# Two linear-attention blocks behind one gate: how B's reciprocals reach the partitions that scale with them

## The chip, the cores and the metric

The kernel runs on one core of one Trainium2 chip. The metric is the device time of one execution in microseconds; the times shown are medians of several runs. A core has a matrix engine (TensorE; PE in the profile, its weight loads PEld), a vector engine (VectorE, DVE), a scalar engine (ScalarE, ACT), GpSimd (POOL) and SyncE (SP), which here only issues DMA transfers. All five run their own instruction streams in order and wait for each other by semaphores.

## The reference

Two blocks A and B of linear attention work on the same x (2048 rows of 640), each with 32 heads of 20 columns, and a gate mixes them row by row:

```python
x = A_x
g = _sigmoid((x * gate_w).sum(-1, keepdims=True))
a = _A_ref(x, A_wqkv, A_wo)
b = _B_ref(x, B_wqkv, B_wo)
return g * a + (1 - g) * b

# each block, for every head:
pq, pk = phi(q), phi(k)      # phi(t) = where(t > 0, t + 1, exp(t)) + 1e-6
kv  = einsum("bhsd,bhse->bhde", pk, v)
z   = einsum("bhsd->bhd", pk)
num = einsum("bhqd,bhde->bhqe", pq, kv)
den = einsum("bhqd,bhd->bhq", pq, z)[..., None] + 1e-6
o   = num / den              # then all heads side by side, @ wo
```

Inputs and output are bf16.

## The kernel before, in words

The rows are cut in 16 tiles of 128. The kernel never forms v or the attention output: it computes G = x^T phi(k), from it kv = wv^T G for each head, and M = kv wo (640 by 640, one for each block, called M_A and M_B), so that the output is the sum over both blocks of (phi(q) / den, weighted by the gate) times M. phi(q) lies transposed in `pqT[0]` (A) and `pqT[1]` (B): five chunks of 128 columns by 2048 rows. Its columns are dealt out in a mixed order, so that partition p of every chunk belongs to head p // 4. One row of reciprocals per head therefore serves four neighbouring partitions.

**The reciprocals.** `Den.mm` multiplies phi(q) by the heads' sums of phi(k). The result has one partition for each of four groups of 512 rows and each of 32 heads. `ln`, `rec` and `ex` make `rT` of it, 128 partitions by 512, the gate divided by the denominator. `R` holds the same numbers spread out: partition p has the 2048 values of head p // 4, in four parts j of 512 rows. `scale(b, m, part)` multiplies chunk m of `pqT[b]` by R on VectorE, over all rows or over `part`. There is one R: A's values are in it first, and B's overwrite them after A's last scaling, `scale(0, 4)`.

- For A, `norm_load` (L976) stores rT four times over to DRAM (`r_rows`, 512 KB) and loads it back into R. It follows `ex2` in a list of steps called PLAN, at about 65 us.
- For B, `norm_spread` (L983) does it on the chip: four matmuls with a 0/1 matrix `spread` as weights (L988), and two ScalarE copies from PSUM into R (L992).

**Around it.** `g_strassen(1, ...)` (L736) computes G of block B by the Strassen-Winograd scheme from seven products `g_prod`, each with 16 matmuls. Instructions of VectorE, ScalarE and SyncE are written between the products by hand, in the order in which these engines execute them. `m_a(g, slot)` and `m_b(g, banks)` make six row blocks of M_A and M_B; each is copied from PSUM and stored to DRAM (`m_rows`, L878). M_A is then loaded back in the layout that the last product wants (L764), M_B in two loads (`m_load`, L899). M_A's tile `M[0]` is also the place where its blocks stand before they are stored. `load_wo(1, ...)` loads B's output weights in three transfers (L1121 twice, L1124).

**The last product** is again a Strassen-Winograd scheme, over rows 0 to 1023 (`SH` = 1024) and the rest, A and B, and the column halves of M. `p_diff(rows)` makes D3, the difference of A's two row halves; `p_sums(rows, ks)` makes sums of A's and B's scaled halves (k = 1: lower halves A + B, in place in `pqT[0]`; 2 and 4: into xT). `tm_first` makes TM[0] = M_A's right half minus its left, `m_sum(k)` TM[1] to TM[3], which need M_B. `part[0..3]` are row quarters of 256 rows within each half. Eight `Pair`s of row tiles run products `p1` to `p7`: p1 needs A's upper rows and M_A; p5 needs sum 1 and TM[0]; p2 needs B's scaled upper rows and M_B; p7 needs D3 and TM[2]; p6 needs sum 2 and TM[1]; p4 needs B's scaled lower rows and TM[3]; p3 needs sum 4 and M_B.

SyncE's queue before, from 116 us on: stores of M_A's blocks 0 to 5, the load of M_A (it waits for those stores to land), three loads of wo, stores of M_B's blocks 0 to 5, two loads of M_B, and the stores of the output.

Of the kernel before, what the change touches and what calls it, by code (L numbers as in the profile page):

```python
# [9 lines left out]
P = 128  # L10
FP32 = mybir.dt.float32
BF16 = mybir.dt.bfloat16
# [3 lines left out]
S, D, H = 2048, 640, 32  # L16
# [39 lines left out]
def kernel(  # L56
# [52 lines left out]
    def ps(name, slot=None):  # L109

        return banks(ps_raw(name, slot))
# [11 lines left out]
    zE = persist.tile([P, 2 * D], BF16, name="zE")  # L123
    E4 = zE[:, D:2 * D]
    maskE = persist.tile([P, HF], BF16, name="maskE")
    spread = persist.tile([P, P], BF16, name="spread")
    R = persist.tile([P, 4, HB], BF16, name="R")
    kv6 = [persist.tile([P, D], BF16, name="kvA6")[:], zE[:]]
    lift = persist.tile([P, 1], FP32, name="lift")
# [27 lines left out]
    scratch = ctx.enter_context(tc.tile_pool(name="scratch", bufs=1, space=bass.MemoryType.DRAM))  # L157
    m_rows = scratch.tile([D, D], BF16, name="m_rows")
    g_rows = scratch.tile([2 * ST, P], FP32, name="g_rows")
    r_rows = scratch.tile([4, P, HB], BF16, name="r_rows")  # L160

    wq_dram = [A_wqkv.rearrange("(c p) f -> p c f", p=P), B_wqkv.rearrange("(c p) f -> p c f", p=P)]
    wo_dram = [A_wo, B_wo]
# [37 lines left out]
    for r in range(4):  # L201
        rows = slice(32 * r, 32 * r + 32)
        nc.gpsimd.tensor_copy(out=I4[rows], in_=ident[rows, rows])
    nc.gpsimd.tensor_copy(
        out=spread[:].rearrange("p (h t) -> p h t", t=TW), in_=I4[:, :, None].to_broadcast([P, H, TW])
    )
    nc.gpsimd.memset(maskE[:], 1.0)
    for lo in range(0, HF, K6):
        part = maskE[:, lo:min(lo + K6, HF)]
# [526 lines left out]
    def g_strassen(b, main, second, spare, rest=None):  # L736

        x11, x12 = [xn[:, k:k + hc, 0:ic] for k in (0, hc)]
        x22 = xn[:, hc:ST, ic:2 * ic]
        b11 = pk[:, 0:hc, 0:HF]  # L740
        b21, b22 = [pk[:, hc:ST, n * HF:(n + 1) * HF] for n in range(2)]
        lo, hi = GT

        def temp(name):
            return work.tile([P, 2, HF], FP32, tag="osb", name=name, bufs=3)

        def add(dst, pt, sb):
            nc.vector.tensor_tensor(out=dst, in0=pt[:, :, 0:HF], in1=sb[:], op=ALU.add)

        even, odd = ps("gs0", main), ps("gs1", second)  # L750
        sel = []
        g_prod(even, x11, b11, True)
        nc.scalar.copy(out=odd[:, :, 0:HF], in_=even[:, :, 0:HF])
        if b == 0:
            rest()
            zr = z_rows(0, spare)
            sq_sum(1, 0)
            g_prod(even, x12, b21, False)
            nc.scalar.copy(out=lo[:, 0:2, :], in_=even[:, :, 0:HF])
            sq_sum(2, 0)  # L760
            x_sum(3)
        else:
            m_a(5, 2)
            nc.sync.dma_start(out=M[0][:], in_=m_rows[:].rearrange("(p m) d -> p m d", m=DT))  # L764
            load_wo(1, nc.sync)
            scale(0, 3)
            zr = z_rows(1, spare)
        g_prod(odd, SX[2], TK[b][2], False, lambda: sel.append(z_pass(b, zr)))
        u2 = temp("u2")
        nc.scalar.copy(out=u2[:], in_=odd[:, :, 0:HF])  # L770
        if b == 1:
            scale(0, 4)
            p_diff(part[0])
            rts = rec_pass(b, sel[0], 2)
            k_sum(1, 1)
            for rows in part[1:3]:
                p_diff(rows)
            g_prod(even, x12, b21, False)
            nc.scalar.copy(out=lo[:, 0:2, :], in_=even[:, :, 0:HF])
            norm_spread(b, rts, (2, spare))  # L780
        else:
            k_sum(0, 1)
            norm_load(rec_pass(b, sel[0], 2))
            x_sum(4)
            for k in (3, 4):
                sq_sum(k, 0)
            tq_sums(1, (0, 1))
        g_prod(odd, SX[3], TK[b][3], False)
        u3 = temp("u3")
        nc.scalar.copy(out=u3[:], in_=odd[:, :, 0:HF])  # L790
        if b == 1:
            for rows, ms in ((slice(0, SH), (0, 1)), (slice(SH, S), (0, 1))):
                for m in ms:
                    scale(b, m, rows)
        even = ps("gs0", main)
        g_prod(even, SX[1], TK[b][1], True)
        add(hi[:, 2:4, :], even, u3)
        if b == 0:
            tq_sums(1, (2, 3))
        else:  # L800
            scale(b, 2)
            scale(b, 3)
        g_prod(odd, x22, TK[b][4], False)
        nc.scalar.copy(out=lo[:, 2:4, :], in_=odd[:, :, 0:HF])
        for ns in ((0, 1),) if b == 0 else ((0,), (1,)):
            g_prod(even, SX[4], b22, False, None, ns)
            for n in ns:
                nc.vector.tensor_tensor(out=hi[:, n, :], in0=even[:, n, 0:HF], in1=u2[:, n], op=ALU.add)
            if b == 1 and ns == (0,):
                rest()  # L810

    def z_rows(b, slot=None):

# [66 lines left out]
    def m_a(g, slot):  # L880

        pt = ps("mA", slot)
        to = m_block(0, g, cells(pt), M[0][:, g, :] if g < DT else None)
        n = to.shape[0]
        nc.scalar.copy(out=to.rearrange("p (b n) -> p b n", b=2), in_=pt[:n, :, 0:HF])
        m_store(g, to)
# [43 lines left out]
    def rec_pass(b, zsel, slot):  # L930

        d = Den(b, lambda: ps(f"den{'AB'[b]}", slot)[:, 0, :])
        d.mm(zsel)
        for go in (d.ln, d.rec, d.ex) if b == 0 else (d.ln,):
            for n in range(2):
                go(n)
        if b == 1:
            for n in range(2):
                d.rec(n)
                d.ex(n)  # L940
        return d.rT
# [4 lines left out]
    def p_diff(rows):  # L946

        up = slice(SH + rows.start, SH + rows.stop)
        add_rows(D3[:, :, rows], pqT[0][:, :, rows], pqT[0][:, :, up], ALU.subtract)
# [12 lines left out]
    def tm_first(cs):  # L962
        add_rows(TM[0][:, cs], M[0][:, cs, HF:D], M[0][:, cs, 0:HF], ALU.subtract)
# [9 lines left out]
        else:  # L973
            add_rows(TM[3][:], b[:, :, lo], TM[1][:], ALU.subtract)

    def norm_load(rT):  # L976

        nc.sync.dma_start(
            out=r_rows[:].rearrange("j (h t) n -> (j h) t n", t=TW), in_=rT[:, None, :].to_broadcast([P, TW, HB])
        )  # L980
        nc.sync.dma_start(out=R[:], in_=r_rows[:].rearrange("j p n -> p j n"))

    def norm_spread(b, rT, slots):  # L983

        pts = [ps(f"ex{'AB'[b]}", s) for s in slots]
        for j in range(4):
            rows = slice(32 * j, 32 * j + 32)
            nc.tensor.matmul(  # L988
                pts[j // 2][:, j % 2, :], lhsT=spread[rows, :], rhs=rT[rows, :], start=True, stop=True,
            )  # L990
        for jj in range(2):
            nc.scalar.copy(out=R[:, 2 * jj:2 * jj + 2, :], in_=pts[jj][:])  # L992

    def scale(b, m, part=slice(0, S)):

        rec = R[:].rearrange("p j n -> p (j n)")
        nc.vector.tensor_tensor(out=pqT[b][:, m, part], in0=pqT[b][:, m, part], in1=rec[:, part], op=ALU.mult)
# [119 lines left out]
    def load_wo(b, eng):  # L1117
        wo_sb[b] = wpool.tile([P, 2, 3, D], BF16, tag="wo", name=f"wo{'AB'[b]}")
        halves = wo_dram[b].rearrange("(h r) f -> h r f", h=2)
        for h in range(2):  # L1120
            eng.dma_start(  # L1121
                out=wo_sb[b][:K6, h, 0:2], in_=halves[h, 0:2 * K6].rearrange("(j p) f -> p j f", p=K6)
            )
        eng.dma_start(out=wo_sb[b][:HF - 2 * K6, :, 2], in_=halves[:, 2 * K6:HF].rearrange("h p f -> p h f"))  # L1124
# [68 lines left out]
    with tc.manual_schedule():  # L1193
# [166 lines left out]
        for name in PLAN.split():  # L1360
            steps[name]()
            if name == "ex2":
                norm_load(den.rT)
        t1 = wpool.tile([P, hc, HF], BF16, tag="wk", name="T1")
        TK[1][1] = t1[:]
        for k in (3, 2, 4):
# [12 lines left out]
        def kv_low():  # L1379
            kv = cells(ps("kvB", 2))  # L1380
            kv_mm(1, kv, range(3))
            kv_mask(1, kv, 0, 2)
            kv_mask(1, kv, 2, 3)
            tm_first(slice(0, 3))

        g_strassen(1, 1, 0, 3, kv_low)
        new_stage(None)
# [11 lines left out]
            kv_mm(1, [None, acc["x"][g > 3]], [g], (2, 3, 4, 0, 1))  # L1399
        for g in range(3, 6):  # L1400
            kv_mask(1, [None, acc["x"][g > 3]], g, g + 1)
        pairs[4].p1(acc["w"][0], (0, 1))
        m_b(3, [acc["w"][1], acc["x"][0]])
        pairs[4].p1(acc["w"][0], (2,))
# [2 lines left out]
        pairs[4].p1(acc["w"][0], (3, 4))  # L1407
        pairs[4].p1_out()
        m_load(0, 3, nc.sync)
        m_load(3, 6, nc.sync)  # L1410
        tm_first(slice(3, DT))
        scale(1, 4)
        for rows, ks in ((0, (1,)), (1, (1,)), (2, (1,)), (0, (2, 4))):
            p_sums(part[rows], ks)
        for k, to in ((5, None), (6, acc["x"][0]), (7, acc["w"][1]), (2, acc["z"][0]), (3, acc["z"][1])):
            pairs[k].p1(to)
        held["p5"] = wpool.tile([P, 4, HF], FP32, tag="wv", name="p5s")
        pairs[0].p1()
        pairs[2].p5(spare[0])
        pairs[3].p5(acc["w"][1])  # L1420
        pairs[1].p1()
        pairs[4].p5(spare[0])
        pairs[5].p5(acc["z"][1])
        for p in pairs[0:2]:
# [2 lines left out]
        inner = ctx.enter_context(late_pool("inner"))  # L1427
        acc["y"] = [bank(inner, f"oy{n}") for n in range(2)]
        TM[3] = wpool.tile([P, DT, HF], BF16, tag="wk", name="TM3")
        p_sums(part[1], (2, 4))  # L1430
        p_diff(part[3])
        for k in (2, 1, 3):
            m_sum(k)
        for p in pairs[0:2]:
            p.p2()
            p.c11()
        for p in pairs[0:2]:
            p.p7()
            p.p6()
            p.c22()  # L1440
        pairs[0].p4()
        pairs[0].p3()
        later = {1: (2, (2,)), 2: (2, (4,)), 4: (3, (2,)), 5: (3, (4,))}
# [51 lines left out]
```

## Time and profile before

| | us |
|---|---|
| runs | 182.61, 183.02, 183.47 |
| median | 183.02 |
| the profiled execution | 182.66 |
| its span on the core | 180.9 |
| TensorE busy | 176.9 |
| TensorE weight loads (beside the matmuls) | 117.6 |
| VectorE busy | 150.6 |
| ScalarE busy | 104.8 |
| GpSimd busy | 5.0 |

The profile is of one execution. A line of its timeline has the start in us from the beginning of the span, the duration in us, the engine, the line of the kernel, the operation, out<-in by the program's names, shapes and the count of instructions merged, and in brackets the idle time before it with what ended it. A line of waits has the total, the count and the longest. A line of DMA issues has the KB of each and the median time from issue to landing. SPq stands for an issue by SyncE; its duration is that of the issue, not of the transfer. In a line of windows the columns are the stretch, its length, busy us of PE, PEld, DVE, ACT and POOL with counts, TensorE's granted clock, the DMA engines' share and GB/s. A tile's name may be that of its storage: `zE` holds B's kv blocks, `SQ` holds D3, `xT` some of the sums.

### The profile page before, as it was taken

The numbers are of one execution on the slowest core, as the hardware profiler recorded it, in microseconds if no ns is written. First come the engines' busy times: TensorE is split into PE (matmuls) and PEld (weight loads), VectorE is DVE, ScalarE is ACT, GpSimd is POOL, SyncE is SP. The second block draws the span as 40 slices with busy tenths as digits, with TensorE's granted clock in tenths as the row PEclk, the third lists the DMA queues.
The fourth block names the chain that finished last, engine by engine and source line by source line (L and its number), as shares of the span: only waits on it lengthen the run. The fifth ranks groups of instructions, "written<-read, shape, count | busy, mean of one in ns | idle before, by whom it ended". The sixth has DMA issues, their size and how long they took to land.

```text
span 180.9 us, 3378 instructions
## 1 busy us (share of the span) xinstructions
PE 176.9 (98%) x1282; PEld 117.6 (65%) x1282; DVE 150.6 (83%) x275; ACT 104.8 (58%) x212; POOL 5.0 (3%) x21
## 2 busy tenths in 40 slices
PE   7999999999999999999999999999999999999993
PEld 2666656655666677676666566766678777777772
DVE  0478988999899999998888889987988988687764
ACT  2066579975884434547777695863814755466210
POOL 8300000000000000000000000000000000000000
PEclk9999999999999999999999999999999999999999
DMA  5995448985002634032000000043901560222132
GB/s 176 286 184 92 93 111 264 366 178 150 31 0 85 209 111 135 0 82 99 5 0 0 0 0 5 23 135 101 277 10 42 163 163 0 100 105 90 72 132 89
DMA packets 21602, 18.85 MB, mean 104 GB/s; under 512 B 9298, under 2 KB 21074, under 8 KB 21586
## 3 DMA queue, kind: packets, MB, share of 16 engines
q1 hardware_dynamic: 20722, 17.82, 35.5%
q10 hardware_dynamic: 864, 0.82, 1.5%
q8 instruction: 10, 0.16, 0.4%
q14 instruction: 6, 0.05, 0.1%
HBM read 11.86 MB, written 4.80 MB: 92 GB/s over the span
## 4 chain that ended last, share of the span: by engine, by line
PE 96%; DMA 2%; DVE 1%; issue 0%
PE kA L313 12%; PE kB L313 11%; PE gs L731 9%; PE q L500 9%; PE gs L1251 9%; PE qA L366 7%; PE oy L1008 6%; PE oz L1008 5%; PE ox L1008 5%; PE ow L1008 4%; PE q L431 4%; PE gB L701 2%; PE gA L701 2%; DMA xn<-in_A_x_dram 2%; PE q L366 2%; PE kB L500 1%
## 5 line engine op out<-in xcount | busy, mean ns | idle before, releaser
L313 PEld LDWEIGHTS <-xT 128*128 128x128 bf16 x300 | 28.9, 97 | 14.1 <-DVE xT L271 0.3
L313 PE MATMUL kA<-wkA,xT 128*128 128x320 bf16 (+1 forms) x160 | 23.4, 299 | 0.0
L313 PE MATMUL kB<-wkB,xT 128*128 128x320 bf16 x140 | 20.8, 299 | 0.0
L524 ACT ACTIVATE e<-kB 128x640 bf16<-128x640 f32 (+1 forms) x17 | 11.4, 676 | 9.5 <-PE kB L313 5.7
L282 ACT ACTIVATE e<-kA 128x640 bf16<-128x640 f32 x16 | 11.3, 715 | 7.8 <-PE kA L313 7.8
L524 ACT ACTIVATE e<-q 128x512 bf16<-128x512 f32 x18 | 10.3, 596 | 6.7 <-PE q L500 3.8
L537 DVE SCALAR_TENSOR_TENSOR pk<-kB,e 128x640 bf16<-128x640 f32 (+1 forms) x17 | 13.2, 782 | 0.9
L366 PE MATMUL qA<-xT,wqA 128*128 128x512 bf16 x60 | 13.4, 379 | 0.0
L290 DVE TENSOR_SCALAR e<-e 128x640 bf16<-128x640 bf16 (+2 forms) x28 | 9.6, 346 | 4.0 <-ACT e L282 3.8
L530 DVE TENSOR_SCALAR e<-e 128x640 bf16<-128x640 bf16 (+2 forms) x30 | 9.9, 332 | 2.3 <-ACT e L524 2.3
L366 PEld LDWEIGHTS <-wqA 128*128 128x128 bf16 x64 | 7.5, 117 | 5.9
L1071 ACT COPY u<-ox 128x320 f32<-128x320 f32 x8 | 3.4, 425 | 11.4 <-PE ox L1008 11.4
L1008 PEld LDWEIGHTS <-xT 128*128 128x128 bf16 x85 | 8.1, 98 | 2.9
L1008 PEld LDWEIGHTS <-pqTA 128*128 128x128 bf16 x85 | 8.0, 98 | 2.8
L1013 DVE TENSOR_TENSOR osb<-oz,u 128x320 bf16<-128x320 f32 (+2 forms) x18 | 8.0, 453 | 2.2 <-PE oz L1008 1.8
L1008 PEld LDWEIGHTS <-pqTB 128*128 128x128 bf16 x80 | 7.7, 98 | 3.1 <-DMA MB<-m_rows 0.2
L500 PE MATMUL q<-xT,wqB 128*128 128x512 bf16 x32 | 9.0, 379 | 0.0
L301 DVE SCALAR_TENSOR_TENSOR pk<-kA,e 128x640 bf16<-128x640 f32 x10 | 8.2, 822 | 0.9
L282 ACT ACTIVATE e<-qA 128x1024 bf16<-128x1024 f32 x6 | 6.2, 1027 | 4.4 <-PE qA L366 4.4
L701 PEld LDWEIGHTS <-xn 128*128 128x128 bf16 x64 | 6.2, 98 | 3.0
L1251 PEld LDWEIGHTS <-xn 128*128 128x128 bf16 x64 | 6.1, 98 | 3.1 <-DVE xn L944 0.4
L731 PEld LDWEIGHTS <-xn 128*128 128x128 bf16 x64 | 6.1, 98 | 2.9 <-issue 0.7
(212 smaller groups left out, 368.5 us busy)
## 6 DMA issues: line engine op xcount, KB each, us to landing
out_dram<-osb SPq DMA_DIRECT2D x14, 160.0 KB, 1.8
xn<-in_A_x_dram SPq DMA_DIRECT2D x3, 640.0 KB, 6.2
wvA<-in_A_wqkv_dram SPq DMA_DIRECT2D x1, 800.0 KB, 10.3
wkB<-in_B_wqkv_dram SPq DMA_DIRECT2D x1, 800.0 KB, 4.6
wqB<-in_B_wqkv_dram SPq DMA_DIRECT2D x1, 800.0 KB, 6.6
wvB<-in_B_wqkv_dram SPq DMA_DIRECT2D x1, 800.0 KB
MA<-m_rows SPq DMA_DIRECT2D x1, 800.0 KB, 6.4
MB<-m_rows SPq DMA_DIRECT2D x2, 400.0 KB, 4.1
```

Source lines behind the costliest of these rows:

```text
L282: nc.scalar.activation(out=to, in_=part, func=ACT.Exp)
L290: nc.vector.tensor_scalar(self.e, self.e, 1.0, EPS, op0=ALU.min, op1=ALU.add)
L313: nc.tensor.matmul(pt[:, hf, 0:n], lhsT=xT[:, c, i * P:(i + 1) * P], rhs=wk[b][:, c, hf * HF:hf * HF + n], start=(c == 0), stop=(c == DT - 1),
L366: nc.tensor.matmul(dst, lhsT=mixed(wq[b][:, c, :], m), rhs=xT[:, c, n * HB:(n + 1) * HB], start=first, stop=last,)
L500: nc.tensor.matmul(dst, lhsT=left(c), rhs=right(c), start=first and k == 0, stop=last and k == len(cs) - 1, skip_group_check=not first,)
L524: nc.scalar.activation(out=self.part(self.e, k), in_=self.srcs[k](), func=ACT.Exp)
L530: nc.vector.tensor_scalar(self.e, self.e, 1.0, EPS, op0=ALU.min, op1=ALU.add)
L537: nc.vector.scalar_tensor_tensor(out=self.part(self.dst, k), in0=src(), scalar=1.0 + EPS, in1=self.part(self.e, k), op0=ALU.add, op1=ALU.max,)
L701: nc.tensor.matmul(pt[:, hf, 0:HF], lhsT=xn[:, i, c * P:(c + 1) * P], rhs=pk[:, i, hf * HF:(hf + 1) * HF], start=(i == 0), stop=(i == ST - 1),
L731: nc.tensor.matmul(pt[:, n, 0:HF], lhsT=left[:, i, n * P:(n + 1) * P], rhs=right[:, i, :], start=(first and i == 0), stop=(i == hc - 1), s ...
L1008: nc.tensor.matmul(dst, lhsT=left[:, c, r0:r0 + P], rhs=right[:, c, :], start=(first and c == 0), stop=(c == DT - 1), skip_group_check=not ...
L1251: nc.tensor.matmul(dst[n], lhsT=left[:, i, n * P:(n + 1) * P], rhs=right[:, i, :], start=(first and i == 0), stop=(i == hc - 1), skip_grou ...
```

## The change

- `norm_store` stores rT once (128 KB) and `norm_load` reads it back in four loads, one for each group of 512 rows; each row of DRAM is read by four partitions. A and B have their own DRAM scratch. Both blocks use this; the spread matrix, its matmuls and copies are gone.
- In `g_strassen(1, ...)`, B's wo is loaded ahead of M_A, and the store and loads of the reciprocals follow M_A's load on SyncE's queue.
- `scale` for B is by row halves: the upper halves of chunks 0 to 2 follow the fourth G product, chunk 3 the kv masks, chunk 4 the masks of the second half; the lower halves of all five stand after the loads of M_B.
- `p_diff(part[3])` and the whole of `tm_first` move into `g_strassen(1, ...)`, ahead of the fourth G product.
- M_B is read back in three loads: blocks 0 to 2, blocks 3 and 4, block 5.
- The order of the sums changes (quarters 1, 2, 0 for k = 1), `p_sums(part[1], ...)` moves behind `m_sum`, and the P1 products of pairs 0 and 1 now both stand ahead of the P5 products. Pair 3's P5 uses another bank.

```diff
@@ -157,7 +156,7 @@
-    r_rows = scratch.tile([4, P, HB], BF16, name="r_rows")
+    r_rows = [scratch.tile([4, H, HB], BF16, name=f"r_rows{b}") for b in "AB"]
@@ -761,8 +757,8 @@
             m_a(5, 2)
+            load_wo(1, nc.sync)
             nc.sync.dma_start(out=M[0][:], in_=m_rows[:].rearrange("(p m) d -> p m d", m=DT))
-            load_wo(1, nc.sync)
             scale(0, 3)
@@ -771,16 +767,17 @@
             p_diff(part[0])
-            rts = rec_pass(b, sel[0], 2)
+            norm_store(1, rec_pass(b, sel[0], 2))
+            norm_load(1, range(4))
             k_sum(1, 1)
...
-            norm_spread(b, rts, (2, spare))
...
@@ -789,17 +786,16 @@
         if b == 1:
-            for rows, ms in ((slice(0, SH), (0, 1)), (slice(SH, S), (0, 1))):
-                for m in ms:
-                    scale(b, m, rows)
+            p_diff(part[3])
+            tm_first(slice(0, DT))
         even = ps("gs0", main)
         g_prod(even, SX[1], TK[b][1], True)
         add(hi[:, 2:4, :], even, u3)
...
-            scale(b, 2)
-            scale(b, 3)
+            for m in (0, 1, 2):
+                scale(b, m, slice(0, SH))
         g_prod(odd, x22, TK[b][4], False)
...
                 rest()
+                scale(b, 3, slice(0, SH))
@@ -973,23 +970,16 @@
+    def norm_store(b, rT):
+
+        nc.sync.dma_start(out=r_rows[b][:].rearrange("j h n -> (j h) n"), in_=rT[:])
+
+    def norm_load(b, js):
+
+        for j in js:
+            nc.sync.dma_start(
+                out=R[:, j, :], in_=r_rows[b][j][:, None, :].to_broadcast([H, TW, HB])
+            )
...
@@ -1381,7 +1372,6 @@
             kv_mask(1, kv, 2, 3)
-            tm_first(slice(0, 3))
@@ -1399,6 +1389,7 @@
             kv_mask(1, [None, acc["x"][g > 3]], g, g + 1)
+        scale(1, 4, slice(0, SH))
         pairs[4].p1(acc["w"][0], (0, 1))
@@ -1407,18 +1398,19 @@
         m_load(0, 3, nc.sync)
-        m_load(3, 6, nc.sync)
-        tm_first(slice(3, DT))
-        scale(1, 4)
-        for rows, ks in ((0, (1,)), (1, (1,)), (2, (1,)), (0, (2, 4))):
+        m_load(3, 5, nc.sync)
+        m_load(5, 6, nc.sync)
+        for m in range(DT):
+            scale(1, m, slice(SH, S))
+        for rows, ks in ((1, (1,)), (2, (1,)), (0, (1,)), (0, (2, 4))):
             p_sums(part[rows], ks)
...
-        pairs[0].p1()
+        for p in pairs[0:2]:
+            p.p1()
         pairs[2].p5(spare[0])
-        pairs[3].p5(acc["w"][1])
-        pairs[1].p1()
+        pairs[3].p5(acc["z"][0])
...
-        p_sums(part[1], (2, 4))
-        p_diff(part[3])
         for k in (2, 1, 3):
             m_sum(k)
+        p_sums(part[1], (2,))
...
             p.c22()
+            if p.i == 0:
+                p_sums(part[1], (4,))
```

More of the change, by code (lines that the diff above doesn't have):

```diff
@@ L125 @@
     maskE = persist.tile([P, HF], BF16, name="maskE")
-    spread = persist.tile([P, P], BF16, name="spread")
     R = persist.tile([P, 4, HB], BF16, name="R")
@@ L203 @@
         nc.gpsimd.tensor_copy(out=I4[rows], in_=ident[rows, rows])
-    nc.gpsimd.tensor_copy(
-        out=spread[:].rearrange("p (h t) -> p h t", t=TW), in_=I4[:, :, None].to_broadcast([P, H, TW])
-    )
     nc.gpsimd.memset(maskE[:], 1.0)
@@ L779, in g_strassen @@
             nc.scalar.copy(out=lo[:, 0:2, :], in_=even[:, :, 0:HF])
-            norm_spread(b, rts, (2, spare))
         else:
             k_sum(0, 1)
-            norm_load(rec_pass(b, sel[0], 2))
+            norm_store(0, rec_pass(b, sel[0], 2))
+            norm_load(0, range(4))
             x_sum(4)
@@ L974, in m_sum @@
             add_rows(TM[3][:], b[:, :, lo], TM[1][:], ALU.subtract)
[L976 to L989, printed above, removed]
-            )
-        for jj in range(2):
-            nc.scalar.copy(out=R[:, 2 * jj:2 * jj + 2, :], in_=pts[jj][:])
+    def norm_store(b, rT):
[4 more added lines that the diff above has]
+                out=R[:, j, :], in_=r_rows[b][j][:, None, :].to_broadcast([H, TW, HB])
+            )
     def scale(b, m, part=slice(0, S)):
@@ L1362 @@
             if name == "ex2":
-                norm_load(den.rT)
+                norm_store(0, den.rT)
+                norm_load(0, range(4))
         t1 = wpool.tile([P, hc, HF], BF16, tag="wk", name="T1")
```

## The prediction

> **What bounds the kernel now.** I read the page first: busy times, then the chain of work that ended last.
>
> ```profile
> span 180.9 us, 3378 instructions
> PE 176.9 (98%) x1282; PEld 117.6 (65%) x1282; DVE 150.6 (83%) x275; ACT 104.8 (58%) x212; POOL 5.0 (3%) x21
> ...
> PE 96%; DMA 2%; DVE 1%; issue 0%
> ```
>
> TensorE makes up 96% of the chain, and "issue", the time in which it waits for nothing visible, is 0%. The kernel is bound by TensorE from end to end. An edit can gain only by taking TensorE work away, and it loses when it makes TensorE wait. So I then read the timeline around the edited lines (105 to 154 us), to see which work of VectorE and of the DMA queues ends just before TensorE needs it.
>
> ```profile
> 122.35 0.31 SPq L878 DMA_DIRECT2D m_rows<-m  x1
> ...
> 124.08 0.35 SPq L764 DMA_DIRECT2D MA<-m_rows  x1
> ...
> 124.52 0.88 SPq L1121 DMA_DIRECT2D woB<-in_B_wo_dram  x2
> ...
> 125.45 1.27 SPq L1124 DMA_DIRECT2D woB<-in_B_wo_dram  x1
> ...
> 125.48 2.35 PE L731 MATMUL gs<-pk,xn 128*128 128x320 bf16 x16
> ...
> 126.56 0.78 ACT L928 ACTIVATE rT<-d 128x256 bf16<-128x256 f32 x2
> ...
> 127.76 0.39 PE L988 MATMUL exB<-rT,spread 32*128 32x512 bf16 x4
> ...
> 128.09 2.35 PE L731 MATMUL gs<-xT,xn 128*128 128x320 bf16 x16
> 128.22 1.55 DVE L944 TENSOR_TENSOR SQ<-pqTA 128x1280 bf16<-128x1280 bf16 x2
> ...
> 129.69 2.49 DVE L997 TENSOR_TENSOR pqTB<-pqTB,R 128x1024 bf16<-128x1024 bf16 x4
> ...
> 130.27 2.34 PE L731 MATMUL gs<-T,S 128*128 128x320 bf16 x16
> ```
>
> **What is removed.** The four matmuls of L988 and two ScalarE copies. Sixteen G matmuls without them start 2.18 us before the next sixteen (128.09 to 130.27); with them it is 2.61 us (125.48 to 128.09). So they cost TensorE **0.43 us**, and that is all the change can gain: everything else on TensorE is only reordered. The two copies and GpSimd's copy for the spread matrix lie beside TensorE and count nothing.
>
> **A's spread.** One store of 128 KB and four loads take the place of a 512 KB store and one 512 KB load.
>
> ```profile
> 68.54 0.38 SPq L981 DMA_DIRECT2D R<-r_rows  x1
> ...
> 73.54 2.35 DVE L997 TENSOR_TENSOR pqTA<-pqTA,R 128x2048 bf16<-128x2048 bf16 x2
> ```
>
> ```profile
> MA<-m_rows SPq DMA_DIRECT2D x1, 800.0 KB, 6.4
> ...
> woB<-in_B_wo_dram SPq DMA_DIRECT2D x2, 300.0 KB, 7.4
> m_rows<-MA SPq DMA_DIRECT2D x4, 150.0 KB, 2.0
> ...
> ge<-g_rows SPq DMA_DIRECT2D x4, 128.0 KB, 3.0
> ...
> R<-r_rows SPq DMA_DIRECT2D x1, 512.0 KB, 3.8
> ```
>
> R lands at 72.3 (68.54 + 3.8), 1.2 us before its first use. A smaller store lets the loads start earlier, and they cover four issues as below: nothing, hidden by those 1.2 us; without that cover the price would be what the last load is late.
>
> **B's reciprocals: when do they arrive?** The matmuls gave R on chip; now it takes two transfers in series. rT is ready at 127.34 (126.56 + 0.78), so the store is issued at 127.4. Ahead of it on SyncE's queue stand wo and M_A. The wo loads no longer wait for M_A's stores to land: they go out at 122.7 (122.35 + 0.31), and M_A at about 124.1 as before. Together they are 1,600 KB, which before flowed from 124.1 on; how long shows in the windows:
>
> ```profile
> 130.00:132.00 2.00, 2.00 (x17) 1.47 (x15) 2.00 (x4) 1.08 (x2) 0.00 (x0) 1.00 0.66 147
> 132.00:134.00 2.00, 2.00 (x17) 1.43 (x15) 1.47 (x3) 0.00 (x0) 0.00 (x0) 1.00 0.01 4
> ```
>
> The last two columns are the DMA engines' share and GB/s: they drain at about 131.5 (0.66 of two microseconds after 130). Starting 1.4 us earlier, they would drain near 130.1. Store landing: 129.4 at best (127.4 + 2.0, as A's block stores alone); 131.9 at worst (behind everything, drained no earlier than before, plus 0.4); I take 130.7, just behind the drain. The scalings of the first half of the rows need loads 0 and 1 only.
>
> ```profile
> L261 SPq DMA_DIRECT2D ge<-g_rows x4: 328/424/1325, 55.4 to 57.7; - x4
> ```
>
> These four 128 KB loads are the nearest row: a second issue comes 0.42 us after the first, and each lands in 3.0; a 150 KB store lands in 2.0. I take 2.5. So **R is there at 130.7 + 0.05 + 0.42 + 2.5 = 133.7**; bounds 131.9 (129.4 + 0.05 + 0.42 + 2.0) and 135.4 (131.9 + 0.05 + 0.42 + 3.0); one slow issue (1.3) would make it 136.3. Nothing else waits on SyncE behind these DMAs: the next store comes after 138.
>
> **What VectorE has to do from there.** Until R comes, p_diff of the last rows (0.82) and all of TM[0] (0.99, as TM<-MB,MA of the same size below) are moved into the gap that the scalings leave at 129.8. TM[0] waits for M_A, which lands at 130.5 before (124.08 + 6.4); behind wo I bound it by 129 and 131.5. It then ends by 132.5, and the add at L748 has its input at 132.3 in the new time. At worst 0.2 late, and its reader, the matmuls after x22, has 1 us: nothing.
>
> ```profile
> 132.71 0.82 DVE L748 TENSOR_TENSOR GT<-gs,u 128x640 bf16<-128x640 f32 x1 [0.54 <-PE gs L731]
> ...
> 135.90 0.49 DVE L808 TENSOR_TENSOR GT<-gs,u 128x320 bf16<-128x320 f32 x1
> ...
> 136.64 0.55 DVE L863 TENSOR_TENSOR zE<-kvB,maskE 120x240 bf16<-120x240 f32 x2 [0.24 <-PE kvB L853]
> ...
> 137.53 0.44 PE L869 MATMUL ow<-woB,zE 120*120 120x320 bf16 x2
> 137.73 0.49 DVE L808 TENSOR_TENSOR GT<-gs,u 128x320 bf16<-128x320 f32 x1
> ...
> 138.35 0.90 PE L853 MATMUL ox<-GT,wvB 128*120 128x120 bf16 x15
> ```
>
> Behind R stand, in VectorE's order: three half scalings (0.62 each, 2.49 for four), the L808 add (0.49), the masks (0.55), a fourth half scaling (0.68), the second L808 add (0.49). That is 4.07 us, and the kv matmuls of the upper blocks (138.35, so 137.92 now; their first three of five chunks do not need it, 0.15) want its result. **TensorE does not wait if R is there by 137.92 + 0.15 - 4.07 - 0.1 for the hand-over = 133.9.** Each microsecond later is a microsecond of TensorE, and at 134.3 the gain of 0.43 is gone. With 133.7 the wait is nil, but the margin is 0.2.
>
> **The second half of the scalings.** All five now stand between the masks and the sums.
>
> ```profile
> 140.25 0.49 DVE L893 CAST MBr<-oz 120x320 bf16<-120x320 f32 x1
> ...
> 142.31 2.30 DVE L944 TENSOR_TENSOR pqTA<-pqTA,pqTB 128x1280 bf16<-128x1280 bf16 x3
> ...
> 144.67 0.84 PE L1008 MATMUL mB<-TM,pqTA 128*128 128x320 bf16 x5
> ```
>
> The last copy of M_B ends at 140.74; with a half scaling ahead of it 140.95 to 141.4 (all or none of it absorbed by the earlier start). Five halves make 144.1 to 144.5, the sum of rows 256 to 511 (0.82) 144.9 to 145.3. Its reader, P5 of pair 2, is at 144.67 - 0.43 + 0.68 (pair 1's P1 now goes first) = 144.92. Before, the sums had been done a microsecond earlier. So 0 to 0.4 of waiting; I take 0.15, nearer the lower end, because a free VectorE follows TensorE there.
>
> **M_B in three loads.** The load of blocks 3 and 4 no longer waits for the last store.
>
> ```profile
> 149.42 1.52 PE L1008 MATMUL ow<-MB,pqTB 128*128 128x320 bf16 x10
> 149.46 0.99 DVE L944 TENSOR_TENSOR TM<-MB,MA 128x1600 bf16<-128x1600 bf16 x1 [0.93 <-DMA MB<-m_rows]
> 150.37 2.07 DVE L944 TENSOR_TENSOR TM<-MB,TM 128x1600 bf16<-128x1600 bf16 x2
> ...
> 152.80 0.49 DVE L1013 TENSOR_TENSOR u<-oy,u 128x320 f32<-128x320 f32 x1 [0.36 <-ACT u L1071]
> ...
> 153.50 0.84 PE L1008 MATMUL oy<-TM,pqTB 128*128 128x320 bf16 x5
> ```
>
> Before, M_B lands as TensorE first wants it, 149.4; now it is wanted at 149.14 (0.43 less 0.15 earlier). An issue that waits one store less brings it by some 0.5, to 148.9; bounds 148.4 and 149.4. I count nothing.
>
> The Trainium skill, "DMA: Bandwidth & Descriptors", section "Anatomy of one DMA", speaks against splitting: some 2.0 us are fixed for each DMA, plus bytes over 436 GB/s, a fit on GpSimd's path. For 128 KB that gives 2.3 us, an estimate; it lies between this trace's 2.0 and 3.0. With it R would be there at 133.5 and the sum would be the same.
>
> **Sum.** -0.43 + 0 (A) + 0 (R) + 0.15 (sums) + 0 (M_B) = -0.28. The profiled execution took 182.66 for a span of 180.9, so 182.4; the median of the runs is 183.02, 0.36 above it: **182.75**.
>
> **The rivals.** (1) R comes late. One mechanism: the store's packets wait behind M_A and wo, so that the two hops end after 133.9. For it: wo, issued 0.44 after M_A, lands at 131.9 and M_A at 130.5 (7.4 and 6.4 after their issues), so this queue serves roughly in order of issue. Against: the queue starts 1.4 us earlier. At 135.4 it costs 1.5, so -0.43 + 1.5 + 0.15 = +1.2, **184.2**; with a slow issue 185.1. It turns the sign from 134.2 on, and counts as slower from 135.1.
>
> By the Trainium skill, the same page, "Queues, rings and completion order", each DMA engine takes descriptors in ring order; the landings above agree, and by it the store cannot pass M_A, which is this rival's condition.
>
> (2) M_B lands no earlier, 149.4. Then TensorE waits 0.26, and the sum of L960 that is moved behind TM[1] to TM[3] ends at 149.46 + 0.99 + 2.07 + 0.8 = 153.3, ahead of the add of u3 (152.80 before). P4 of pair 0 (153.50) then starts at 153.9: +0.4, **183.4**. For it: the landing had no slack. Against: a store less to wait for.
>
> (3) Nothing waits: R by 133, sums in time. -0.43, **182.6**.
>
> (4) The change doesn't do what it says: the scalings wait for all four loads, not two. R is then 0.85 later, 134.55: -0.43 + 0.65 + 0.15 = +0.4, **183.4**.
>
> **How the numbers follow.** Forecast 0.38, (1) 0.25, (2) 0.12, (3) 0.17, (4) 0.08. Half a per cent, about what a measurement of this kernel can tell from no change, is 0.92 us. Faster by that needs twice the work that is taken away, so only scatter of the runs (0.4 either way) gives it: 0.05. Slower by that takes (1) with R after 135.1 or a slow issue, 0.15, or two of the waits together, 0.04: 0.19. The rest, 0.76, is within. The range reaches from (3) less scatter, 182.2, to (1) at its bound, 184.2; the forecast's own is 182.3 to 183.2.
>
> **What would show it.** L988 gone, and the start of the G matmuls that followed it 0.43 earlier; R's loads landing at about 133.7, the first scaling right then; TensorE's waits there under 0.1. Wrong if TensorE idles for VectorE between 137 and 138.5 (rival 1), at 145 by over 0.4, or for M_B at 149; or if the chain of waits shows R's DMA.

## The result, and the profile after

| | before | after |
|---|---|---|
| median of 6 runs each, us | 182.97 (182.61 to 183.47) | 185.25 (184.46 to 186.77) |
| ratio, with its 95% interval | | 1.0133 [1.0106, 1.0159] |
| the profiled execution | 182.66 | 186.44 |
| its span | 180.9 | 184.7 |
| its mean granted clock | 1.00 | 0.991 |

The change makes the kernel slower by 1.3%, and 185.25 lies above the predicted range. The page of the changed kernel first: its span and busy times, the granted clock by slices, the queue that fetches instructions (packets, MB, share of 16 engines), and the shares of the chain that ended last.

```profile
span 184.7 us, 3373 instructions
...
PE 178.5 (97%) x1268; PEld 119.7 (65%) x1278; DVE 150.7 (82%) x277; ACT 103.3 (56%) x210; POOL 4.8 (3%) x20
...
PEclk9999999999999999999999999999996999999999
...
q8 instruction: 10, 0.16, 0.4%
...
PE 91%; DMA 4%; DVE 2%; ACT 1%; issue 0%; SPq 0%; DVEq 0%
```

Two things differ from before. TensorE's share of the chain fell from 96% to 91%, and DMA's rose from 2% to 4%: something outside TensorE now sets the pace for a while. And one digit of the granted clock is a 6. The chain, in order of time, says where (start, duration, what):

```profile
126.95 0.79 ACT rT L925 x2
...
127.75 5.24 DMA r_rowsB<-rT
...
133.06 0.53 SPq L980
...
133.65 2.37 DMA R<-r_rowsB
...
136.11 1.90 DVE pqTB L987 x3
138.01 0.41 DVE GT L804
...
138.46 1.63 PE gs L727 x8
```

The chain leaves TensorE at rT and comes back at the last G product, and every step between belongs to B's reciprocals: the store, the issue of two loads, the second load, three half scalings, one add. rT starts 0.39 later than before (126.95 against 126.56) with the same matmuls ahead of it, so **0.39 is taken off below to compare with times of before**. (Line numbers moved too: the G product's L731 is L727 now, L808 is L804, L1008 is L998.)

The DMA issues of the changed kernel (KB of each, us from issue to landing) show which step is long:

```profile
MA<-m_rows SPq DMA_DIRECT2D x1, 800.0 KB, 8.0
...
r_rowsA<-rT SPq DMA_DIRECT2D x1, 128.0 KB, 1.7
...
r_rowsB<-rT SPq DMA_DIRECT2D x1, 128.0 KB, 5.2
```

The two stores are the same instruction on the same 128 KB. A's, with nothing ahead of it, lands in 1.7 us; B's, behind wo and M_A, takes 5.2. M_A itself took 6.4 before, 8.0 now that wo goes first. The timeline shows who waits (brackets: idle time and what ended it):

```profile
123.13 0.88 SPq L1111 DMA_DIRECT2D woB<-in_B_wo_dram  x2
...
124.67 0.35 SPq L761 DMA_DIRECT2D MA<-m_rows  x1
...
132.67 0.99 DVE L941 TENSOR_TENSOR TM<-MA 128x1600 bf16<-128x1600 bf16 x1 [1.78 <-DMA MA<-m_rows]
...
134.57 1.25 PE L727 MATMUL gs<-pk,MB 128*128 128x320 bf16 x8
...
136.11 1.90 DVE L987 TENSOR_TENSOR pqTB<-pqTB,R 128x1024 bf16<-128x1024 bf16 x3 [1.72 <-DMA R<-r_rowsB]
...
138.46 1.63 PE L727 MATMUL gs<-pk,MB 128*128 128x320 bf16 x8 [1.91 <-DVE GT L804]
...
148.99 0.84 PE L998 MATMUL mB<-TM,pqTA 128*128 128x320 bf16 x5
```

VectorE's wait of 1.72 for R becomes TensorE's wait of 1.91 for the add L804. Without a wait the two halves of the last G product start 1.84 us apart (136.77 less 134.93 in the first experiment below); here it is 3.89 (138.46 less 134.57), so **2.05 us are lost**, 1.91 of them idle. More is lost right behind it. The windows of the changed kernel (stretch, length, busy us of PE, PEld, DVE, ACT, POOL, granted clock, DMA share, GB/s):

```profile
136.00:138.00 2.00, 0.56 (x12) 0.46 (x11) 1.89 (x4) 0.00 (x0) 0.00 (x0) 1.00 0.31 99
138.00:140.00 2.00, 1.54 (x9) 1.06 (x9) 1.47 (x5) 0.00 (x0) 0.00 (x0) 0.80 0.00 0
140.00:142.00 2.00, 2.00 (x13) 1.65 (x12) 0.98 (x2) 1.44 (x4) 0.00 (x0) 0.50 0.04 8
142.00:144.00 2.00, 2.00 (x22) 1.82 (x22) 1.35 (x5) 1.13 (x4) 0.00 (x0) 0.85 0.36 99
```

In the two microseconds after the idle stretch the granted clock falls to 0.80, then to 0.50; the trace's clock records have it at 0.50 from 139.19 on, for 3.41 us. From that G product to the first P5 product (148.99) this execution takes 10.53 us. In the profile of e8_after_again, the same kernel with the same wait (138.49 less 134.61 is 3.88) and no fall of the clock behind it, the stretch takes 8.90 (138.49 to 147.39): 1.63 lost to the clock. The span adds up: 0.39 - 0.43 + 2.05 + 1.63 = 3.64 of the 3.8 by which it grew.

### The profile page after: what moved, and what is told of

Read it like the earlier page. It is cut to its first block, busy times and chain, and to the rows that moved or that the text cites. A ratio compares the mean times of both kernels' runs of the same rounds, so it can differ in the third digit from the quotient of the medians.

```text
span 184.7 us, 3373 instructions
## 1 busy us (share of the span) xinstructions
PE 178.5 (97%) x1268; PEld 119.7 (65%) x1278; DVE 150.7 (82%) x277; ACT 103.3 (56%) x210; POOL 4.8 (3%) x20
## 4 chain that ended last, share of the span: by engine, by line
PE 91%; DMA 4%; DVE 2%; ACT 1%; issue 0%; SPq 0%; DVEq 0%
PE kA L309 12%; PE kB L309 10%; PE gs L1241 8%; PE q L496 8%; PE qA L362 7%; PE oy L998 6%; PE oz L998 6%; PE ox L998 4%; PE q L427 4%; PE ow L998 4%; PE gs L727 3%; DMA r_rowsB<-rT 3%; PE gB L697 2%; PE gA L697 2%; PE warm L225 2%; PE q L362 1%
## 5 line engine op out<-in xcount | busy, mean ns | idle before, releaser
L998 PEld LDWEIGHTS <-xT 128*128 128x128 bf16 x85 | 8.1, 98 | 2.9
L998 PEld LDWEIGHTS <-pqTA 128*128 128x128 bf16 x85 | 8.1, 98 | 2.8
L998 PEld LDWEIGHTS <-pqTB 128*128 128x128 bf16 x80 | 7.8, 98 | 3.0
L727 PEld LDWEIGHTS <-xn 128*128 128x128 bf16 x64 | 6.2, 98 | 2.8 <-issue 0.4
```

Of the source, the lines that this page charges most:

```text
L727: nc.tensor.matmul(pt[:, n, 0:HF], lhsT=left[:, i, n * P:(n + 1) * P], rhs=right[:, i, :], start=(first and i == 0), stop=(i == hc - 1), s ...
L998: nc.tensor.matmul(dst, lhsT=left[:, c, r0:r0 + P], rhs=right[:, c, :], start=(first and c == 0), stop=(c == DT - 1), skip_group_check=not ...
```

## The experiments

Theory: B's store waits behind what is queued ahead of it, R comes late, and the last G product pays. Rivals: the other edits cost it; the clock alone costs it; VectorE's new order is what is too tight.

| label | what it is | us, median (range, runs) | before beside it | ratio [95%] |
|---|---|---|---|---|
| e1_wo_last | changed, wo behind R's store and loads | 183.23 (182.46 to 183.54, 10) | 183.06 | 1.0006 [0.9991, 1.0021] |
| e2_chip_spread | changed, B's spread by matmuls again | 183.72 (183.28 to 184.22, 6) | 183.06 | 1.0037 [1.0019, 1.0056] |
| e3_store_act | changed, B's store from ScalarE's queue | 185.32 (184.47 to 185.93, 4) | 183.06 | 1.0127 [1.0093, 1.0161] |
| e4_keep_busy | changed, 14 unread matmuls in the wait | 184.56 (184.34 to 184.98, 4) | 183.06 | 1.0097 [1.0075, 1.0118] |
| e5_two_loads | e1, M_B in two loads | 182.85 (182.50 to 184.88, 12) | 183.12 | 0.9995 [0.9973, 1.0017] |
| e6_cover_mb | e1, more work ahead of M_B's first use | 183.51 (183.36 to 183.98, 11) | 183.12 | 1.0029 [1.0016, 1.0042] |
| e7_dram_only | before, B's spread through DRAM alone | 190.30 (189.17 to 191.26, 4) | 183.12 | 1.0387 [1.0350, 1.0425] |
| e8_after_again | the changed kernel once more | 185.03 (184.02 to 186.36, 6) | 183.12 | 1.0109 [1.0072, 1.0145] |
| e9_wo3_early | e5, the third load of wo early, into its own tile | 182.87 (182.30 to 183.34, 12) | 183.13 | 0.9994 [0.9978, 1.0010] |
| e10_chip_two | e2, M_B in two loads | 183.49 (182.69 to 184.12, 12) | 183.13 | 1.0020 [1.0002, 1.0038] |
| e11_sums_back | e9, two sums back in their old place | 182.81 (182.31 to 183.32, 11) | 182.94 | 0.9986 [0.9972, 1.0001] |

**What the store waits behind.**

```diff
 m_a(5, 2)
-load_wo(1, nc.sync)
 nc.sync.dma_start(out=M[0][:], in_=m_rows[:].rearrange("(p m) d -> p m d", m=DT))
...
 norm_load(1, range(4))
+load_wo(1, nc.sync)
```

> The edit: on SyncE's queue wo goes behind the reciprocals' store and loads (M_A, store, four loads, wo), nothing else. Theory (the queue serves in order of issue, so in the changed kernel the store sat behind wo and M_A and landed 5.2 us after its issue, 127.75 to 132.99): the store is now behind M_A alone and lands about 2.5 us earlier, the first scaling starts at 133 to 134 instead of 136.1, the 1.9 us wait of the G matmuls for the add at L804 shrinks to under 0.5, and the time falls by 1.5 to 2.2 us, unless wo (issued about 132.5, 7 us to land) is late for M_B's blocks at 138, which would give 1 us back. Rival (two DRAM hops take that long anyway): the store lands within 0.5 us of before, the first scaling within 0.5 us of 136, and the time stays within 0.5 us of 185.

The timeline of this kernel; its rT starts at 127.32, 0.76 later than before:

```profile
128.12 0.34 SPq L975 DMA_DIRECT2D r_rowsB<-rT  x1
...
129.90 2.47 SPq L980 DMA_DIRECT2D R<-r_rowsB  x4
...
133.77 1.89 DVE L987 TENSOR_TENSOR pqTB<-pqTB,R 128x1024 bf16<-128x1024 bf16 x3
...
134.93 1.25 PE L727 MATMUL gs<-pk,MB 128*128 128x320 bf16 x8
...
136.77 1.25 PE L727 MATMUL gs<-pk,MB 128*128 128x320 bf16 x8
...
145.76 0.84 PE L998 MATMUL mB<-TM,pqTA 128*128 128x320 bf16 x5
...
147.80 2.20 PE L998 MATMUL oz<-TM,pqTA 128*128 128x320 bf16 x15
...
150.10 1.21 PEld L998 LDWEIGHTS <-pqTB 128*128 128x128 bf16 x10 [0.43 <-issue]
150.12 0.99 DVE L941 TENSOR_TENSOR TM<-MB,MA 128x1600 bf16<-128x1600 bf16 x1 [1.53 <-DMA MB<-m_rows]
150.13 1.52 PE L998 MATMUL ow<-MB,pqTB 128*128 128x320 bf16 x10
```

The store lands by 129.90, 1.8 us after its issue, though M_A still stands ahead of it. R is there before VectorE is free, the scaling and the G product carry no wait, and the time falls by 2.0 us. The theory holds: one move of three DMA issues takes back nearly everything. It doesn't become faster than before, because the 0.43 won in the G products is lost again: 0.29 at M_B (the fifteen matmuls from 147.80 start 0.136 apart, so the next could start at 149.84 and starts at 150.13), and some 0.1 each for wo at 138.49 and at P4 (154.28).

```diff
 def norm_store(b, rT):
-    nc.sync.dma_start(out=r_rows[b][:].rearrange("j h n -> (j h) n"), in_=rT[:])
+    (nc.scalar if b == 1 else nc.sync).dma_start(out=r_rows[b][:].rearrange("j h n -> (j h) n"), in_=rT[:])
```

> The edit: only the store of B's reciprocals is issued from ScalarE's queue; wo, M_A and the four loads stay on SyncE's. Theory (order within one queue): the store no longer waits for M_A's transfer, it lands by 130.5 instead of 133.0; the loads still follow M_A on SyncE's queue, so the first scaling starts at 133.5 to 134.5, and the time falls by 1.3 to 2 us to 183 to 184. Rival (the DMA engines themselves are full, whichever queue): the store lands at 132 or later and the time stays within 0.5 us of 185.

The DMA issues of this kernel, then the store and the G product in its timeline:

```profile
MA<-m_rows SPq DMA_DIRECT2D x1, 800.0 KB, 7.8
...
r_rowsB<-rT ACTq DMA_DIRECT2D x1, 128.0 KB, 5.1
```

```profile
128.30 0.33 ACTq L975 DMA_DIRECT2D r_rowsB<-rT  x1
...
139.15 1.25 PE L727 MATMUL gs<-pk,MB 128*128 128x320 bf16 x8 [2.05 <-DVE GT L804]
```

Another queue doesn't help: 5.1 us instead of 5.2, the same wait, the same time. So "order within SyncE's queue" is not it; the store waits in the DMA engines, which both queues share. The Trainium skill, "DMA: Bandwidth & Descriptors", says in its section "Issuing engines are not separate DMA queues" that DMAs started by different engines run on the same 16 DMA engines; the two rows agree with that.

**What the other edits cost.**

```diff
-norm_store(1, rec_pass(b, sel[0], 2))
-norm_load(1, range(4))
+rts = rec_pass(b, sel[0], 2)
...
+norm_spread(b, rts, (2, spare))
```

> The edit: B's reciprocals are spread by the four matmuls and two ScalarE copies again; everything else stays as changed (wo ahead of M_A, A's store and loads, half scalings, order of the sums, three loads of M_B). Theory (the late R is the whole loss): no wait for the add at L804, time within 0.5 us of the kernel before, 182.5 to 183.5. Rival (part of the loss comes from the other edits: VectorE's later sums, M_A behind wo, M_B's loads): 183.8 or more, with a wait of TensorE at the sums (about 145 us) or M_A's TM[0] (132.6) in the trace.

With R made on chip and all other edits kept, 183.72: the rest of the change costs 0.66 us. In its timeline the largest wait is again at M_B (the line is of the weight loads; the matmuls there are 0.19 late):

```profile
149.64 1.20 PEld L1013 LDWEIGHTS <-pqTB 128*128 128x128 bf16 x10 [0.36 <-DMA MB<-m_rows]
```

The rival "the other edits" is thus worth 0.66 of the 2.28. R's route through DRAM makes up the remaining 1.6, net of the four matmuls that it saves and with the clock's share in it. Of the 0.66 the profile shows 0.19 at M_B and 0.12 at P4; the rest isn't located.

**The clock.**

```diff
 for ns in ((0, 1),) if b == 0 else ((0,), (1,)):
+    if b == 1 and ns == (1,):
+        idle = ps("idle", spare)
+        for k in range(14):
+            nc.tensor.matmul(idle[:, k % 2, 0:HF], lhsT=xT[:, 0, 0:P], rhs=pk[:, 0, 0:HF], start=True, stop=True)
     g_prod(even, SX[4], b22, False, None, ns)
```

> The edit: 14 matmuls of 320 columns whose result nobody reads stand before the last G product, where TensorE idled 2.0 us for the add at L804; they take 1.9 us at full speed. Theory (the granted clock falls to one half behind that idle time in some executions, 0.991 and 0.989 over the span, and this costs 1 to 2 us there): the clock is 1.0 in all runs, none is above 185.6, the median falls by 0.3 to 0.8 us to about 184.5, and matmuls behind the place are 136 ns apart instead of 267. Rival (the clock falls for another reason, by chance of the chip): runs at 0.99 of the clock and 186.5 us still occur, and the median stays at 185.2 or rises.

> The changed kernel once more, for the granted clock. Theory (idle time of 2 us brings the clock to one half in some executions): of the new executions a fifth to a half show a clock of 0.985 to 0.995 and 1 to 2 us more than the others, which lie at 184.4 to 185.5. Rival (the two executions at 0.99 were a chance of that chip or hour): all at 0.998 or above, median 184.9.

The filling matmuls and the G product in the timeline of e4_keep_busy:

```profile
136.08 2.07 PE L805 MATMUL idle<-pk,xT 128*128 128x320 bf16 x14
...
138.03 1.25 PE L727 MATMUL gs<-pk,MB 128*128 128x320 bf16 x8
```

TensorE is busy while it waits, the granted clock is 1.00 in all four executions, and none takes over 184.98. Of the twelve executions of the changed kernel three (two of the six beside the result, one of the six here, where I expected a fifth to a half) have a mean granted clock of 0.989 to 0.991, at 186.36, 186.44 and 186.77. The other nine (0.998 to 1.00) have a median of 184.81. The clock therefore adds some 1.7 us to one execution in four. At that rate four executions without a fall come by chance one time in three, so e4_keep_busy alone doesn't show that the filling is the remedy. That the fall goes with the wait is seen in the kernels without it: none of the 74 executions of e1, e2, e5, e6, e9, e10 and e11 is under 0.998. The clock is no rival for the main loss: the nine without it are still 1.7 to 1.8 over the 182.97 and 183.12 of before, and -0.43 + 2.05 = 1.62 is nearly all of that.

**VectorE's order.**

```diff
-rts = rec_pass(b, sel[0], 2)
+norm_dram(rec_pass(b, sel[0], 2))
...
-norm_spread(b, rts, (2, spare))
```

> The edit, on the kernel before: B's reciprocals go through DRAM (one store, four loads, behind M_A and wo on SyncE's queue); scalings, sums, M_B's loads and wo's place stay as before. Theory (R comes at 135 to 136 whenever the store is behind 1,600 KB, and what waits is everything behind the scalings on VectorE): now four half scalings stand ahead of the add at L744, so TensorE waits at the product after x22 from 134.2 until about 139, and the time is 187 to 188.5. Rival (VectorE's new order in the change is what costs, not R): less than 185.

The waits of this kernel (total, count, longest):

```profile
DVE pqTB L1005 <- DMA R<-r_rowsB: 6.6, 1, 6.6
...
PE gs L732 <- DVE GT L749: 5.5, 1, 5.5
```

In the old order of VectorE, all row halves of two scalings stand ahead of an earlier add, and the late R costs TensorE 5.5 us instead of 1.9, and the clock in all four executions (0.981 to 0.990). It came out some 2 to 3 us dearer than I expected, 1.8 of it by that clock in the profile (0.50 from 137.22 for 6.83 us, with TensorE busy for 3.52 of them). The scalings by row halves and the moved sums are therefore not what makes TensorE wait for R; they are what kept that wait near 2 us. A part of the 0.66 above may still be theirs.

**M_B.** From e1_wo_last on, the question was why the gain of 0.43 doesn't arrive.

```diff
 m_load(0, 3, nc.sync)
-m_load(3, 5, nc.sync)
-m_load(5, 6, nc.sync)
+m_load(3, 6, nc.sync)
```

> The edit, on the kernel with wo behind the reciprocals: M_B read back in two loads as before, not three. In that kernel TensorE is 0.43 us early until M_B, then waits about 0.3 us for it (149.99, as late as in the kernel before), and ends level with the kernel before. Theory (M_B's landing is set by its last store and by the transfer of 800 KB, not by the number of loads): last landing within 0.3 us, time within 0.4 us of the three-load kernel's 183.2. Rival (the third load, issued 0.4 us later, is what comes last): M_B lands 0.3 us or more earlier and the time falls to 182.9 or below.

> The edit, on e2 (B's spread on the chip, all else as changed): M_B read back in two loads as before. Theory (of e2's 0.66 us over the kernel before, most is M_B landing late through the third load): the wait at M_B (0.19 us) and at P4 (0.12 us) go, time 182.9 to 183.4, within 0.3 us of the kernel before. Rival (it is the half scalings and the later sums): 183.5 or more.

The DMA issues of e1_wo_last (three loads), then of e5_two_loads:

```profile
MB<-m_rows SPq DMA_DIRECT2D x1, 400.0 KB, 4.2
...
MB<-m_rows SPq DMA_DIRECT2D x1, 100.0 KB, 5.1
```

```profile
MB<-m_rows SPq DMA_DIRECT2D x2, 400.0 KB, 3.8
```

The last 100 KB, behind the other two loads, take longer from issue to landing than 400 KB. Two loads are better by 0.4 (e5 against e1, the medians taken against the kernel before beside them; 0.2 by the ratios) and by 0.3 (e10 against e2). The intervals overlap, so the sign rests on the two pairs agreeing. With two loads e10 is still 0.36 over the kernel before, more than I expected, so by these medians the third load is less than half of the 0.66. M_B's landing also moves between executions: TensorE has no wait for it in the profile of e5_two_loads, and 0.3 in that of e9_wo3_early, which loads M_B in the same way.

```diff
-for rows, ks in ((1, (1,)), (2, (1,)), (0, (1,)), (0, (2, 4))):
+for rows, ks in ((1, (1,)), (2, (1,)), (0, (1,)), (0, (2, 4)), (3, (1,)), (1, (2,))):
     p_sums(part[rows], ks)
...
+pairs[6].p5(spare[1])
```

> The edit, on the kernel with wo behind the reciprocals: P5 of pair 6 (0.68 us of TensorE that came later) is moved ahead of the first product that needs M_B, with its sum (quarter 3, k = 1) and the sum 2 of quarter 1 ahead of TM[2], where VectorE idled 1.5 us for M_B. Theory (the gain of 0.43 us is given back at M_B): the wait of 0.3 us at M_B disappears, P4 does not wait either, time 182.6 to 183.0, 0.1 to 0.4 us under the kernel before. Rival (the gain is not there, or VectorE is short instead): time within 0.1 us of 183.2, with a new wait of TensorE between 150 and 155.

The waits of this kernel:

```profile
DVE u L1003 <- ACT u L1061: 2.0, 3, 0.8
...
PE oy L998 <- DVE u L1003: 0.4, 1, 0.4
```

The wait for M_B is gone, and TensorE waits 0.4 for VectorE instead. The time didn't fall as expected: 183.51, no better than e1.

```diff
 wv[1] = load_w(1, "v", nc.sync)
+held["wo3"] = wpool.tile([P, 2, D], BF16, tag="wo3", name="wo3B")
+load_wo3(1, held["wo3"][:HF - 2 * K6], nc.sync)
```

> The edit, on the kernel with wo behind the reciprocals and two loads of M_B: the quarter of wo that blocks 2 and 5 need (200 KB) goes into a tile of its own and is loaded at about 80 us, where SyncE's queue is idle. Theory (what is left of the 0.43 us after e5 is a wait of 0.13 us for wo, which landed at 137.75 as TensorE wanted it): that wait vanishes, nothing else changes, time 182.5 to 182.9, 0.2 to 0.5 us under the kernel before. Rival (a wait of another kind takes its place at the same spot, for the masks): time as in e5 within 0.05 us, the gap at 138 us stays.

```diff
+p_sums(part[1], (2, 4))
 for k in (2, 1, 3):
     m_sum(k)
-p_sums(part[1], (2,))
```

> The edit, on e9: the sums 2 and 4 of quarter 1 go back ahead of TM[2] to TM[3], where VectorE idles 1.6 us for M_B. Theory (P4's wait of 0.13 us came from these sums standing behind TM[3]): the wait at P4 (154 us) vanishes, the one at M_B (0 to 0.4 us, as M_B happens to land) stays, time 182.5 to 182.9. Rival (VectorE is then late for TM[2] itself): a wait at P7, time 183 or more.

Both take away a wait of 0.13 (for wo at 137.89 in e5, and for P4's input at 154.15 in e9), which is too little to see in the medians: 182.87 and 182.81. In the profile of e11 a wait of 0.16 at 151.40, ahead of P6, stands in its place. The last is the best version: 0.13 under the kernel before beside it, with an interval that just reaches 1. It can't be told from no change.

## Why the prediction was wrong

**The step that failed: "Store landing … I take 130.7, just behind the drain", and with it "R is there at 133.7".** The store landed at 132.6 (132.99 - 0.39), past even the bound of 131.9. Everything around it was right: wo issued at 122.7, the store at 127.4, and from the landing to the first scaling 3.1 us (132.99 to 136.11) against the 2.97 that the terms gave. So the error of R, 135.7 instead of 133.7, is the error of the store. The bound for M_A (129 to 131.5) failed with it: M_A landed at 132.28 (132.67 - 0.39).

What I had read as the drain is a mean over 16 DMA engines; a DMA lands with the last of them. In the profile of before itself the last packet of wo starts at 132.34, 0.8 after the 131.5 that I read from the windows. The packet records of the changed kernel's profile show the rest: of the store's 128 packets of 1 KB, 120 have started by 130.85 and ended by 130.90. The last eight, one engine's share, start from 132.19 to 132.48, right after the last eight packets of M_A (130.30 to 131.93). The landing follows 0.46 after the end of the last packet (132.53 to 132.99). By the same 0.46 the 120 would have landed at 131.36, 130.97 in times of before (an estimate), 0.3 after my 130.7: the one late engine makes 1.6 of the error of 1.9. The bounds should have come from the landing of the last transfer ahead, not from the windows' share.

**Rival 1 was the right mechanism with too low a price and chance.** I gave it a wait of 1.5 at R's bound of 135.4; with R at 135.7 the wait was 2.05, because the **threshold** was off as well. I named the kv matmuls of the upper blocks as first waiter and 133.9 as the limit. The first waiter is the second half of the last G product: it writes the PSUM tile `even`, whose other half the add L804 still has to read, and the add stands behind three half scalings. R had to be there by 136.11 - 2.05 - 0.39 = 133.7. No row of before shows this wait, since the add was never late there; the code does: the loop over the two halves has the add of one half between the products, on one tile. No run gives the halves tiles of their own.

**Not foreseen: the clock.** A wait had its own length as price. Here it also costs about 1.7 us in one execution of four.

**"An issue that waits one store less brings it by some 0.5": wrong.** In e1_wo_last the loads go out earlier than before by 0.6 (143.40 - 0.76 against 143.24), but M_B is there at 149.3 against 149.4. The forecast that counted nothing for M_B was near for the wrong reason; the condition of rival 2 ("M_B lands no earlier") is what happens, and it eats 0.29 of the 0.43.

**Right.** The four matmuls are worth 0.43: in e1_wo_last the last G product starts at 136.77, 136.01 in times of before, against 136.45. A's spread is hidden (1.7 us for the store). TM[0] waits 1.78 for M_A, yet the matmuls after x22 follow without a gap (134.57). The sums cost about 0.1 (gaps in the profiles of e1_wo_last and e2_chip_spread), though at P4 and not at P5 of pair 2. The scalings wait for two loads, not four: rival 4 is out.

**Open.** Why that one engine is late. A fetch of 16 KB of instructions (q8 on the page) fits closely. In all six profiles with wo ahead of M_A it starts at 127.0 to 128.0 and takes 1.3 to 1.4 us, and the last ten packets of wo begin within 0.02 of its end (128.98 against 128.99 in the changed kernel). The last eight of M_A, and of the store where there is one, follow those ten. With M_A ahead of wo the fetch starts at 124.8 to 125.6. No run moves the fetch alone, and why it comes later behind wo isn't known. e1_wo_last takes away both the bulk and the late engine; that the bulk alone is enough is seen in e7_dram_only, where the fetch is over at 126.86 and the store, behind wo, still takes 5.7 us to land.

## What to carry to other kernels

A small transfer in a chain waits for what is queued ahead of it on the DMA engines, on either of the two queues tried here (5.2 and 5.1 us against 1.7 with nothing ahead): issue the bulk that isn't urgent behind it (here the move of one line, 2.0 us). Take its landing from the landing of the last transfer ahead, not from the mean share of the engines. And for each wait look for the first reader or writer of the same PSUM tile, not of the same values.

## What was not expected of the hardware

**A wait of 2 us can halve TensorE's clock.** In the windows above the clock reads 0.50 after 1.91 us of idling. This happened in three of twelve executions of the changed kernel, in none of the four of e3_store_act, whose profile shows 2.05 us of idling, in none of e4_keep_busy, where the wait is filled, and in all four of e7_dram_only with 5.5 us. The Trainium skill, "TensorE: Matmul & The Clock Gate", section "Part 1: The HAM clock gate", has the clock fall to one half after an idle window of some 3.4 us, and says that these windows run freely. The length agrees with the clock records here: the half clock lasts 3.41 us in the changed kernel and 6.83, twice that, in e7_dram_only. That the window is idle throughout doesn't agree: in the 3.41 us before the fall TensorE was busy for 1.50 in the changed kernel (135.78 to 139.19) and for 1.25 in e7_dram_only (133.81 to 137.22), and here the measurement decides.

Windows that run freely can also explain why the same wait sometimes counts and sometimes doesn't. In the trace of e8_after_again, where the clock stayed at 1.00 behind the wait, 177.49 us lie between the first clock record and the fall at 182.54, near the end of the span: 52 times 3.413. Counted back thirteen times, a window ends at 138.17, inside the wait (136.59 to 138.49), and holds only 1.58 of it; TensorE is busy for 1.84 there. In the changed kernel one window holds all 1.91. So few profiles don't prove the limit.

**Issue on another queue is no way past.** The store from ScalarE's queue landed 5.1 us after its issue at 128.30. In the packet records of e3_store_act its first packet starts at 130.26, as M_A's first completion record comes, and its last eight from 132.58 on, as M_A's last packet ends. The Trainium skill, "DMA: Bandwidth & Descriptors", section "Queues, rings and completion order", says that each DMA engine takes turns between queues, a packet of typically some 9 to 17 descriptors at a time. No such turn is seen here; but with 128 pieces in all M_A has only eight on each of 16 engines, which one such packet may hold, so this run doesn't contradict the page.
